# The last output copied in two column halves, a branch hint ahead of the end, and four accumulator banks for the last group

## The chip, the core and the metric

The kernel runs on one core of a Trainium2 chip. The engines that compute are TensorE (PE in the profile; its weight loads are PEld), VectorE (DVE), ScalarE (ACT) and GpSimd (POOL); SyncE (SP) issues the transfers. The metric is the device time of one execution in microseconds. A kernel's time is the median of its runs.

## What is computed

A gated linear recurrence over 768 steps for 4 x 8 heads of width 48, followed by a feed-forward layer on its output (3072 tokens, 384 wide, 2048 hidden):

```python
f = 1.0 / (1.0 + np.exp(-f_logit))
for t in range(S):
    state = f[:, :, t, :, None] * state + np.einsum('bhd,bhe->bhde', k[:, :, t], v[:, :, t])
    y[:, :, t] = np.einsum('bhd,bhde->bhe', q[:, :, t], state)
x = y.transpose(0, 2, 1, 3).reshape(B * S, H * D)
h = x @ w_in
g = h * np.tanh(np.log1p(np.exp(h)))      # for h > 20: h * tanh(h)
out = g @ w_out
```

## The kernel before

**Recurrence.** The sequence is cut into 24 chunks (6 in time, 4 batches) of 128 steps. A chunk is four steps in the code: `attn0` (loads `l`, `k`, `q`, `v`, the decays on ACT and DVE, the scores), `attn1`, `attn2`, `attn3` (the outputs, written as a high and a low part into `xt`). Its matmuls write the PSUM tiles `at0`, `at1`, `at2`.

**Feed-forward.** The tokens form 6 groups of 512 columns, the hidden width 16 blocks. One pair of group and block is a unit, 96 in all. A unit is `moe_in` (9 matmuls, L234, into a PSUM tile `h`), `mish` (nine steps, L244 to L252: four ACT passes, three DVE passes, then the high part `gh` on ACT and the low part `gl` on POOL), and `moe_out` (9 matmuls, L257, three into each of the PSUM tiles `o0`, `o1`, `o2`). There are two tiles `h`, two each of `n` and `g`, three each of `gh` and `gl`. The weights of a block are loaded once (`raw`, 768 KB) and split into a high and a low part (`split_w`, L336 to L346) on ACT and DVE. When a group is done, `out_unit` copies `o0` and `o2` with DVE (L619) and `o1` with ACT (L615) into `ob`, and SP sends each copy to `out` (L621). All transfers are issued from SP.

**What sets the order.** No engine's order is written by hand. Each step is added to a `Plan` with its engine, an assumed cost, and the names of what it reads and writes. `order()` packs all steps several times, forwards and backwards, then tries 100 variations of the ranks drawn from a fixed seed, keeps the best by its own model, and issues every engine's instructions in that order. So a step with another cost or another dependence can move instructions anywhere in the program. While the model sees PE idle before the first `moe_out`, it issues matmuls with zeros (`idle`, L326).

**The end.** A general path, for data whose decays are too strong, follows the planned part. `check` counts the good decays into `flag`; at L656 every engine loads `flag` into a register, at L657 it branches past the general path, whose instructions lie in between. After the branch each engine waits for its own work (SP for the eight semaphores of the transfers) and then for the others (L798).

Of the kernel before, what the change touches and what calls it, by code (L numbers as in the profile page):

```python
# [2 lines left out]

# [10 lines left out]
AF = mybir.ActivationFunctionType  # L14
# [5 lines left out]
P = 128  # L20
# [7 lines left out]
GT = GC * C  # L28
NG = NT // GT
NF = DFF // P  # L30
NK = DM // P
# [15 lines left out]
class Plan:  # L47
# [12 lines left out]
    def add(self, engine, cost, issue, reads=(), writes=(), size=0, port=False):  # L60

        n = len(self.steps)
        before = {self.writer[r] for r in reads if r in self.writer}
        for w in writes:
            before |= set(self.readers.get(w, ()))
            before |= {self.writer[w]} if w in self.writer else set()
        for r in reads:
            self.readers.setdefault(r, []).append(n)
        for w in writes:
            self.writer[w], self.readers[w] = n, []  # L70
        before.discard(n)
        self.steps.append((engine, cost, issue, before, size, port or engine == "pool"))
# [117 lines left out]
def recurrence_moe_kernel(  # L190
# [12 lines left out]
    nc = tc.nc  # L203
# [5 lines left out]
    def ctile(shape, dtype, name):  # L209
        return const.tile(shape, dtype, tag=name, name=name)  # L210
# [13 lines left out]
    flag = ctile([1, 1], I32, "flag")  # L224
# [5 lines left out]
    def moe_in(h, xt, j, wih=wih, wil=wil):  # L230
        n = 0
        for a in range(NK):
            for w, x in ((wih, 0), (wih, 1), (wil, 0)):
                nc.tensor.matmul(  # L234
                    h, w[:, j, a * P : (a + 1) * P], xt[:, x, a, :], start=(n == 0), stop=(n == 3 * NK - 1)
                )
                n += 1


    def mish(h, n, g, gh, gl):  # L240

# [20 lines left out]
    with tc.tile_pool(name="work", bufs=1) as pool, tc.tile_pool(  # L262
        name="psum", bufs=1, space=PSUM
    ) as psum:
        def ring(name, n, shape, dtype=F32, space=pool):
            return [space.tile(shape, dtype, tag=f"{name}{i}", name=f"{name}{i}") for i in range(n)]

        l_, k_, q_ = (ring(nm, NR, [P, NP, C]) for nm in "lkq")
# [5 lines left out]
        xt_ = ring("xt", 2, [P, 2, NP, GT], F32R)  # L274
        n_, g_ = (ring(nm, 2, [P, GT]) for nm in "ng")
        gh_, gl_ = (ring(nm, 3, [P, GT], F32R) for nm in ("gh", "gl"))
        ob_ = ring("ob", 3, [P, GT])
        raw_ = ring("raw", 2, [P, W_TILE, 2], I32)
        wt_ = ring("wt", 2, [P, W_TILE], I32)
        at_, h_, o_ = (ring(nm, n, [P, GT], F32, psum) for nm, n in (("at", 3), ("h", 2), ("o", NK)))  # L280
# [3 lines left out]
        add = plan.add  # L284
# [3 lines left out]
        def pairs(name, ps=range(NP)):  # L288
            return [(name, p) for p in ps]
# [277 lines left out]
        units = [(t, g, j) for t, (g, j0, j1) in enumerate(turns) for j in range(j0, j1)]  # L567

        def attend_goal(u):

            per = 4 * GC
            goal = per
            for a, b in LEAD + [(NF * g - 2, NF * (g + 1) - 2) for g in range(2, NG - 1)]:
                goal += min(per, max(0, per * (u + 1 - a) // (b - a)))
            return goal
# [13 lines left out]
        def out_unit(u):  # L589
            t, g, j = units[u]  # L590
            half = g < 2
            first, last = (j == x for x in (turns[t][1], turns[t][2] - 1))
            part = last and half and j == NF - 1
            gs = u % 3
            if part:
                for m in range(NK):
                    add("sp", 500, lambda m=m, g=g: nc.sync.dma_start(ob_[m], halves[g][m * P : (m + 1) * P, :]),
                        [("half", g, m)], pairs(("ob", m)), 262)
            if u == 0:
                plan.until = len(plan.steps)  # L600
            if last or first:
                for m in range(NK):
                    add("pe", 702, lambda m=m: moe_out(o_[m], m, gh_[gs], gl_[gs], j, first, last),
                        [("w", "h", j), ("w", "l", j), ("gh", gs), ("gl", gs)], [("o", m)])
            else:
                add("pe", 2106, lambda: [moe_out(o_[m], m, gh_[gs], gl_[gs], j, first, last) for m in range(NK)],
                    [("w", "h", j), ("w", "l", j), ("gh", gs), ("gl", gs)], [("o", m) for m in range(NK)])
            if last:
                dst = halves[g] if j < NF - 1 else out[:, g * GT : (g + 1) * GT]
                for m in range(NK):  # L610
                    if part:
                        add("dve", T_DVE(GT), lambda m=m: nc.vector.tensor_tensor(ob_[m], o_[m], ob_[m], ALU.add),
                            [("o", m)], pairs(("ob", m)))
                    elif m == 1:
                        add("act", T_ACT(GT, True), lambda m=m: nc.scalar.activation(ob_[m], o_[m], AF.Copy),  # L615
                            [("o", m)], pairs(("ob", m)))
                    else:

                        add("dve", T_DVE(GT), lambda m=m: nc.vector.tensor_copy(ob_[m], o_[m]),  # L619
                            [("o", m)] + ["flag"] * (u == len(units) - 1), pairs(("ob", m)))  # L620
                    add("sp", 500, lambda m=m, dst=dst: nc.sync.dma_start(dst[m * P : (m + 1) * P, :], ob_[m]),  # L621
                        pairs(("ob", m)), [("half", g, m) if half else ("out", g, m)], 262)

        split = 0
        for u in range(len(units) + LAG):
            if u < len(units):
                t, g, j = units[u]
                if j == split:
                    split_w(j)
                    split += 1  # L630
                x, hs, us, gs = g % 2, u % 2, u % 2, u % 3
                xk = [(hl, ("xt", x, c), p) for hl in "hl" for c in range(GC) for p in range(NK)]
                h = h_[hs]
                add("pe", 2106, lambda h=h, x=x, j=j: moe_in(h, xt_[x], j), xk + [("w", "h", j), ("w", "l", j)], [("h", hs)])
                kh, kn, kg = ("h", hs), ("n", us), ("g", us)
                ops = mish(h, n_[us], g_[us], gh_[gs], gl_[gs])
                rw = (
                    ([kh], [kn]), ([], [kn]), ([], [kn]), ([kh, kn], [kg]), ([kn], [kh]), ([], [kh]),
                    ([kh], [kg]), ([kg], [("gh", gs)]), ([kg, ("gh", gs)], [("gl", gs)]),
                )  # L640
                for (e, c, shared, fn), (r, w) in zip(ops, rw):
                    add(e, c, fn, r, w, port=shared)
            while done < min(4 * NCH, attend_goal(u)):
                attend()
            if u == len(units):
                check()
            if u >= LAG:
                out_unit(u - LAG)

        plan.idle = idle  # L650
        with tc.manual_schedule():
            plan.issue()


    total = P * NCH * NP
    good = nc.values_load(flag[0:1, 0:1], min_val=0, max_val=total)  # L656
    with tc.If(good < total):  # L657


        xs = dram.tile([DM, NT], F32, tag="xs", name="xs")  # L660
        with tc.tile_pool(name="slow", bufs=1) as pool, tc.tile_pool(
# [9 lines left out]
            with tc.For_i(0, B, 1) as b:  # L671
                with tc.For_i(0, NP, 1) as p:
                    f, k, q = (st([P, NCB, C], nm) for nm in ("sf", "sk", "sq"))
# [7 lines left out]
                    with tc.For_i(0, D, 1) as e:  # L681
# [13 lines left out]
                        for i in range(2):  # L695
                            ps = psum.tile([2, S // 2], F32, tag=f"sp{i}", name=f"sp{i}")
                            s = slice(i * S // 2, (i + 1) * S // 2)
# [9 lines left out]
            with tc.For_i(0, NG, 1) as g:  # L707
                x = st([P, NK, GT], "sx")
# [10 lines left out]
                n, g_ = (st([P, GT], nm) for nm in ("sn", "sg"))  # L719
                gh, gl = (pool.tile([P, GT], F32R, tag=nm, name=nm) for nm in ("sgh", "sgl"))  # L720
# [82 lines left out]
```

## Time and profile before

| | us |
|---|---|
| median of 3 runs | 522.92 |
| lowest, highest | 519.78, 523.32 |
| the profiled execution's own time | 521.81 |
| its span in the profile | 520.0 |
| PE, DVE, ACT busy of the span | 506.1, 370.4, 415.1 |
| granted TensorE clock | 0.999 |

The span runs from the first to the last instruction; 1.8 us of the execution lie outside it. "Idle before" in a row is the time in which the engine did nothing just ahead of the instructions of the row, with what ended it. A name with q (SPq, DVEq) is the engine's sequencer: it loads registers, branches and waits. A matmul's busy time overlaps the next one's.

### The profile page before, as it was taken

To read this page: it belongs to the slowest core of one execution; us is meant where nothing else is said; L and a number is where in the kernel's file an instruction comes from. 1 tells how busy PE (TensorE), PEld (TensorE's weight loads), DVE (VectorE), ACT (ScalarE), POOL (GpSimd) and SP (SyncE) were. 2 spreads that over 40 slices of the span, in tenths; PEclk is the share of its full clock that TensorE was granted. 3 is DMA by queue.
4 is the path that set the end of the run, shared out by engine and by line. 5 is a ranking of instruction groups with operands and counts; after the bars stand their busy time and mean duration, and the time that the engine had idled before them with its cause. 6 is when DMAs were issued, how large, how long until landed. Compare 5 with 4: busy or idle time off the path is not lost.

```text
span 520.0 us, 12828 instructions
## 1 busy us (share of the span) xinstructions
PE 506.1 (97%) x5258; PEld 399.3 (77%) x5258; DVE 370.4 (71%) x592; ACT 415.1 (80%) x731; POOL 155.1 (30%) x134
## 2 busy tenths in 40 slices
PE   8889899999999999999999999999999999999995
PEld 6667678777778778777777778778787787878884
DVE  3799999999998876856767667675667564554451
ACT  6888888988989978888778788877778785777771
POOL 1321533333322323233223222323231222232321
PEclk9999999999999999999999999999999999999999
DMA  8977534524601633411213321130220000010001
GB/s 278 335 236 261 202 122 154 161 83 140 220 18 34 201 100 98 134 57 33 82 33 94 111 78 45 43 97 17 61 64 1 3 2 32 0 61 1 1 1 66
DMA packets 22625, 48.86 MB, mean 94 GB/s; under 512 B 2656, under 2 KB 3808, under 8 KB 22560
## 3 DMA queue, kind: packets, MB, share of 16 engines
q1 hardware_dynamic: 22560, 47.98, 28.1%
q8 instruction: 42, 0.69, 0.6%
q14 instruction: 23, 0.19, 0.1%
HBM read 39.32 MB, written 6.29 MB: 88 GB/s over the span
## 4 chain that ended last, share of the span: by engine, by line
PE 73%; DVE 11%; ACT 8%; issue 3%; DMA 3%; SPq 1%; DVEq 0%; ACTq 0%
PE h L234 32%; PE o L257 32%; DVE g L250 2%; PE at L457 2%; PE at L504 2%; PE at L492 2%; DVE n L246 2%; DVE g L247 2%; DVE wt L341 2%; DMA l<-ft 1%; PE at L414 1%; PE at L439 1%; DMA raw<-ww 1%; ACT h L248 1%; ACT n L244 1%
## 5 line engine op out<-in xcount | busy, mean ns | idle before, releaser
L252 POOL TENSOR_TENSOR gl<-g,gh 128x512 fp32r<-128x512 f32 x96 | 128.2, 1336 | 294.3 <-ACT gh L251 262.7
L234 PE MATMUL h<-xt,wh 128*128 128x512 f32 x576 | 185.0, 402 | 1.6 <-DVE g L250 1.5
L234 PEld LDWEIGHTS h<-xt,wh 128*128 128x128 f32 x576 | 104.9, 188 | 29.2 <-DVE g L250 4.7
L257 PE MATMUL o<-gh,wh 128*128 128x512 f32 x288 | 116.2, 403 | 0.0
L234 PE MATMUL h<-xt,wl 128*128 128x512 f32 x288 | 113.7, 395 | 0.0
L257 PE MATMUL o<-gh,wl 128*128 128x512 f32 x288 | 113.7, 395 | 0.0
L257 PE MATMUL o<-gl,wh 128*128 128x512 f32 x288 | 113.7, 395 | 0.0
L246 DVE SCALAR_TENSOR_TENSOR n<-n 128x512 f32<-128x512 f32 x96 | 67.1, 699 | 59.8 <-ACT n L245 59.7
L244 ACT ACTIVATE n<-h,hcap 128x512 f32<-128x512 f32 x96 | 65.8, 685 | 34.2 <-PE h L234 33.4
L250 DVE TENSOR_TENSOR g<-g,h 128x512 f32<-128x512 f32 x96 | 65.4, 681 | 33.5 <-ACT h L249 32.9
L248 ACT ACTIVATE h<-n,two 128x512 f32<-128x512 f32 x96 | 66.0, 687 | 18.6 <-DVE g L247 18.6
L251 ACT ACTIVATE gh<-g 128x512 fp32r<-128x512 f32 x96 | 60.3, 628 | 19.2 <-DVE g L250 15.2
L247 DVE TENSOR_TENSOR g<-h,n 128x512 f32<-128x512 f32 x96 | 66.1, 689 | 8.7 <-POOL gl L252 1.3
L245 ACT ACTIVATE n<-n,hcap 128x512 f32<-128x512 f32 x96 | 69.2, 721 | 2.2
L257 PEld LDWEIGHTS o<-gh,wh 128*128 128x128 f32 x288 | 54.0, 187 | 13.6 <-issue 0.3
L257 PEld LDWEIGHTS o<-gl,wh 128*128 128x128 f32 x288 | 54.0, 187 | 13.3
L234 PEld LDWEIGHTS h<-xt,wl 128*128 128x128 f32 x288 | 54.0, 187 | 13.2
L257 PEld LDWEIGHTS o<-gh,wl 128*128 128x128 f32 x288 | 54.1, 188 | 12.0
L249 ACT ACTIVATE h<-h 128x512 f32<-128x512 f32 x96 | 56.0, 583 | 1.7
L383 DVE TENSOR_TENSOR_SCAN cum<-go,l 128x512 f32<-128x512 f32 x20 | 26.7, 1334 | 0.0
L420 DVE TENSOR_TENSOR a<-at,causal 128x256 f32<-128x256 f32 x44 | 17.8, 417 | 9.7 <-PE at L414 9.5
L520 POOL TENSOR_TENSOR state<-tmp,ends 128x256 f32<-128x256 f32 x20 | 16.7, 835 | 21.6 <-PE at L492 17.4
(103 smaller groups left out, 504.4 us busy)
## 6 DMA issues: line engine op xcount, KB each, us to landing
raw<-ww SPq DMA_DIRECT2D x16, 768.0 KB, 4.9
v<-vn SPq DMA_DIRECT2D x24, 256.0 KB, 3.8
k<-kk SPq DMA_DIRECT2D x23, 256.0 KB, 3.3
q<-qq SPq DMA_DIRECT2D x23, 256.0 KB, 3.8
l<-fl SPq DMA_DIRECT2D x20, 256.0 KB, 2.7
out<-ob SPq DMA_DIRECT2D x18, 256.0 KB, 2.6
xt<-xt SPq DMA_DIRECT2D x15, 128.0 KB, 2.1
half<-ob SPq DMA_DIRECT2D x6, 256.0 KB, 2.5
```

The lines of the kernel that those rows point to most:

```text
L234: nc.tensor.matmul(h, w[:, j, a * P : (a + 1) * P], xt[:, x, a, :], start=(n == 0), stop=(n == 3 * NK - 1))
L244: ("act", T_ACT(GT, True, 1), 0, lambda: nc.scalar.activation(u, h, AF.Relu, bias=hcap, scale=-1.0)),
L245: ("act", T_ACT(GT, False, 1), 0, lambda: nc.scalar.activation(u, u, AF.Exp, bias=hcap, scale=-1.0)),
L246: ("dve", T_DVE(GT), 1, lambda: nc.vector.scalar_tensor_tensor(n, u, 2.0, u, ALU.add, ALU.mult)),
L247: ("dve", T_DVE(GT), 0, lambda: nc.vector.tensor_tensor(g, h, n, ALU.mult)),
L248: ("act", T_ACT(GT, False, 1), 0, lambda: nc.scalar.activation(h, n, AF.Ln, bias=two)),
L249: ("act", T_ACT(GT, True), 0, lambda: nc.scalar.activation(h, h, AF.Exp, scale=-1.0)),
L250: ("dve", T_DVE(GT), 0, lambda: nc.vector.tensor_tensor(g, g, h, ALU.mult)),
L251: ("act", T_ACT(GT), 0, lambda: nc.scalar.activation(gh, g, AF.Copy)),
L252: ("pool", T_POOL(GT), 1, lambda: nc.gpsimd.tensor_tensor(gl, g, gh.bitcast(F32), ALU.subtract)),
L257: nc.tensor.matmul(o, w[:, j, m * P : (m + 1) * P], x, start=(first and i == 0), stop=(last and i == 2))
L383: add("dve", 2 * T_DVE(w) - 70, lambda s=s, cum=cum: nc.vector.tensor_tensor_scan(cum.rearrange("p a c -> p (a c)"), go[:, s].rearrange("p ...
```

## The change

Four edits, all in the planned part:

- In the last group's last unit the copy of `o2` becomes two copies of 256 columns. ACT copies the upper half and issues its transfer from its own queue; DVE copies the lower half, SP issues that transfer. Both steps now name `flag` as read; before, only the two full copies on DVE did. The three `moe_out` parts of that unit are tied to the order `o0`, `o1`, `o2`.
- In the last group (units 80 to 95) four tiles serve as `h` (the two and `at0`, `at1`), four as `n` (with `l0`, `l1`) and four as `g` (with `k0`, `k1`).
- The general path gets a name, and a hint that the branch past it is likely taken is placed on ACT, DVE and POOL behind the first instruction each has in the last unit's `mish`, and on SP behind the first transfer of the group before the last.
- The plan is made anew with these steps.

```diff
@@ out_unit
+            end = u == len(units) - 1
...
-                        [("w", "h", j), ("w", "l", j), ("gh", gs), ("gl", gs)], [("o", m)])
+                        [("w", "h", j), ("w", "l", j), ("gh", gs), ("gl", gs)] + [("o", m - 1)] * (end and m > 0), [("o", m)])
...
+                    elif end and m == NK - 1:
+
+                        def part_out(eng, s, m=m, dst=dst):
+                            if eng is nc.sync:
+                                nc.vector.tensor_copy(ob_[m][:, s], o_[m][:, s])
+                            else:
+                                nc.scalar.activation(ob_[m][:, s], o_[m][:, s], AF.Copy)
+                            eng.dma_start(dst[m * P : (m + 1) * P, s], ob_[m][:, s])
+
+                        for e, t_copy, eng, x in (("act", T_ACT(GT // 2, True), nc.scalar, 1), ("dve", T_DVE(GT // 2), nc.sync, 0)):
+                            add(e, t_copy, lambda eng=eng, x=x: part_out(eng, slice(x * GT // 2, (x + 1) * GT // 2)),
+                                [("o", m), "flag"], [("ob", m, x)])
+                        continue
                     else:
-
                         add("dve", T_DVE(GT), lambda m=m: nc.vector.tensor_copy(ob_[m], o_[m]),
-                            [("o", m)] + ["flag"] * (u == len(units) - 1), pairs(("ob", m)))
-                    add("sp", 500, lambda m=m, dst=dst: nc.sync.dma_start(dst[m * P : (m + 1) * P, :], ob_[m]),
+                            [("o", m)], pairs(("ob", m)))
+                    add("sp", 500, partial(mark, "sp" if g == NG - 2 else "", lambda m=m, dst=dst: nc.sync.dma_start(dst[m * P : (m + 1) * P, :], ob_[m])),
...
+        free = NF * (NG - 1)
+        hs_ = [(h, ("h", i)) for i, h in enumerate(h_)] + [(at_[i], ("at", i)) for i in range(2)]
...
+        def mark(e, fn):
+            ins = fn()
+            marks.setdefault(e, ins)
...
-                x, hs, us, gs = g % 2, u % 2, u % 2, u % 3
+                us = u % 2 if u < free else u % 4
+                x, gs = g % 2, u % 3
...
+                    if u == len(units) - 1:
+                        fn = partial(mark, e, fn)
...
+        for e, ins in marks.items():
+            if e:
+                with tc.issue_after(ins.ins):
+                    tc.mark_branch_hint_location("general", "LikelyTaken", engines=[ins.ins.engine])
...
-    with tc.If(good < total):
+    with tc.If(good < total, label="general"):
```

Line numbers in the changed program are one higher up to L592, and 2 to 36 higher behind it. Three places show what the new plan moves. First SP, at the start of the program (`l` decays' inputs, `raw` a weight block, `k`, `q`, `v` a chunk's inputs). Before:

```order
L355 DMA l_82<-ft 128x512
L355 DMA k_84<-kk 128x256
L355 DMA q_87<-qq 128x256 x2
L358 DMA v_90<-vn 128x512
L336 DMA raw_122<-ww 128x1536
L355 DMA k_85<-kk 128x512
L355 DMA l_83<-ft 128x512
L355 DMA q_88<-qq 128x512
```

Now:

```order
L356 DMA q_87<-qq 128x256 x2
L359 DMA v_90<-vn 128x512
L356 DMA l_83<-ft 128x512
L337 DMA raw_122<-ww 128x1536
L356 DMA k_85<-kk 128x512
L356 DMA q_88<-qq 128x512
```

The third chunk's `l_83` is now issued ahead of the first weight block; before, it stood behind it.

Second DVE, around the first unit's last pass (`g` with the tile `h`, L250, now L251). Before:

```order
L346 TENSOR_TENSOR wl_62<-wt0_124,wh_61 128x768 [waits Activation_49]
L250 TENSOR_TENSOR g0_111<-g0_111,h0_129 128x512 [waits Activation_49]
L537 TENSOR_TENSOR xt1_108<-at1_127,xt1_108 128x2x128 [waits Activation_49]
L246 SCALAR_TENSOR_TENSOR n1_110<-n1_110 128x512
L341 SCALAR_TENSOR_TENSOR wt1_125<-raw1_123,wt1_125 128x768 [waits DMAHW5_49,DVE_49]
L537 TENSOR_TENSOR xt1_108<-at0_126,xt1_108 128x2x128 [waits Activation_49]
L247 TENSOR_TENSOR g1_112<-h1_130,n1_110 128x512 [waits DVE_49]
```

Now:

```order
L247 SCALAR_TENSOR_TENSOR n1_110<-n1_110 128x512 [waits Activation_49]
L341 TENSOR_SCALAR wt1_125<-wt1_125 128x768
L251 TENSOR_TENSOR g0_111<-g0_111,h0_129 128x512 [waits DVE_49,Activation_49]
L344 SCALAR_TENSOR_TENSOR wt0_124<-raw0_122,wt0_124 128x768
L476 TENSOR_TENSOR tmp1_106<-at1_127,mid1_104 128x256 [waits DVE_49,PE_49,Pool_49]
L248 TENSOR_TENSOR g1_112<-h1_130,n1_110 128x512 [waits DVE_49]
L421 TENSOR_TENSOR a3_102<-at1_127,causal_66 128x256
```

The second unit's first pass (`n1`) and its second (`g1`) have moved ahead of passes of the weight split and of `xt`. Counted over the whole list, the last pass of units 0 to 9 was DVE's row 69, 79, 85, 96, 100, 114, 117, 124, 130 and 137; now it is row 65, 72, 80, 90, 98, 111, 117, 122, 127 and 134. At unit 19 it is row 195 in both. On ACT the `gh` of units 0 to 9 was row 91, 102, 106, 119, 123, 135, 137, 148, 155 and 163, and is now row 89, 97, 107, 116, 124, 134, 141, 147, 154 and 162.

Third the end, DVE and then ACT. DVE before:

```order
L250 TENSOR_TENSOR g1_112<-g1_112,h1_130 128x512 [waits DVE_49,Activation_49]
L619 COPY ob0_119<-o0_131 128x512 [waits DMAHW0_49,PE_49]
L619 COPY ob2_121<-o2_133 128x512 [waits DMAHW2_49,PE_49]
L656 TENSOR_LOAD flag_71 [waits DVE_49]
```

Now:

```order
L834 BRANCH_PREFETCH_HINT
L251 TENSOR_TENSOR k0_84<-k0_84,at0_126 128x512 [waits DVE_49,Activation_49]
L248 TENSOR_TENSOR k1_85<-at1_127,l1_82 128x512 [waits DVE_49,Pool_49]
L251 TENSOR_TENSOR k1_85<-k1_85,at1_127 128x512 [waits DVE_49,Activation_49]
L588 CAST flag_71<-at2_128 1x1 [waits PE_49]
L633 COPY ob0_119<-o0_131 128x512 [waits DMAHW1_49,PE_49]
L623 COPY ob2_121<-o2_133 128x256 [waits DMAHW2_49,Activation_49]
L692 TENSOR_LOAD flag_71 [waits DVE_49]
```

ACT before:

```order
L251 ACTIVATE gh2_115<-g1_112 128x512 [waits DVE_49,PE_49,Pool_49]
L615 ACTIVATE ob1_120<-o1_132 128x512 [waits DMAHW1_49,PE_49]
L656 TENSOR_LOAD flag_71 [waits DVE_49]
```

Now:

```order
L252 ACTIVATE gh2_115<-k1_85 128x512 [waits DVE_49,PE_49,Pool_49]
L617 ACTIVATE ob1_120<-o1_132 128x512 [waits DMAHW0_49,PE_49]
L625 ACTIVATE ob2_121<-o2_133 128x256 [waits DMAHW2_49,PE_49]
L626 DMA out<-ob2_121 128x256 [waits DMAHW5_49,Activation_49]
L692 TENSOR_LOAD flag_71 [waits DVE_49]
```

DVE's half copy waits for ACT's half copy, not for PE; the cast of `flag` has moved from the middle of the last group to just ahead of DVE's last copies.

In the middle of the program the order of PE has changed too: at the first `moe_out` matmul of a unit, the `moe_in` of 3 more units than of finished `moe_out` had been issued in 27 of units 0 to 31 before (of 4 in five), and of 4 to 6 in 31 of the 32 units 48 to 79; now it is 3 in 26 of these 32 and 4 in six. The zero matmuls of L326 are 29 (before: 32).

## Rows read from the trace of the kernel before

**Rows 1.** The page, its first part: busy time, share of the span and instructions of an engine.

```profile
PE 506.1 (97%) x5258; PEld 399.3 (77%) x5258; DVE 370.4 (71%) x592; ACT 415.1 (80%) x731; POOL 155.1 (30%) x134
```

**Rows 2.** Busy time by stretch: the stretch, its length, then busy us and instructions of each engine, the granted clock, the DMA engines' share and GB/s.

```profile
26.00:65.00 39.00, 35.39 (x783) 27.21 (x771) 38.06 (x60) 32.63 (x64) 13.10 (x11) 1.00 0.69 233
65.00:160.00 95.00, 94.50 (x693) 73.59 (x670) 91.12 (x129) 84.85 (x142) 31.54 (x23) 1.00 0.38 124
...
160.00:514.10 354.10, 354.07 (x3472) 281.04 (x3470) 226.30 (x377) 278.22 (x484) 104.13 (x85) 1.00 0.17 54
...
100.00:150.00 50.00, 49.87 (x346) 39.25 (x345) 48.18 (x66) 43.71 (x70) 16.33 (x12) 1.00 0.43 137
200.00:250.00 50.00, 50.00 (x545) 39.78 (x544) 34.78 (x60) 40.63 (x72) 14.12 (x12) 1.00 0.24 75
```

**Rows 3.** What PE waited for between 26 and 160 us, the first two lines: us in total, times, longest.

```profile
PE h L234 <- DVE g L250: 1.5, 4, 0.8
PE o L533 <- ACT xt L530: 0.8, 1, 0.8
```

**Rows 4.** The zero matmuls (L326) alone, by stretch: PE's busy time and records (two a matmul), then PEld's.

```profile
26.00:40.00 14.00, 5.50 (x22) 3.81 (x22) 1.00 0.72 240
40.00:65.00 25.00, 4.69 (x18) 2.72 (x16) 1.00 0.68 229
65.00:100.00 35.00, 0.00 (x0) 0.00 (x0) 1.00 0.40 133
```

**Rows 5.** The chain of work that ended last, followed back from 30 us: start, us, what. The load `l<-ft` is `l_83`.

```profile
5.45 7.22 DMA l<-ft
12.69 1.04 DVE l L373
...
14.41 0.72 ACT l L375
15.15 0.60 ACT kt L442
```

**Rows 6.** The timeline near the end, the first and the last step of the last unit's `mish`: start, us, engine, line, instruction.

```profile
503.60 0.69 ACT L244 ACTIVATE n<-h,hcap 128x512 f32<-128x512 f32 x1 [0.65 <-PE h L234]
...
509.93 1.29 POOL L252 TENSOR_TENSOR gl<-g,gh 128x512 fp32r<-128x512 f32 x1 [0.65 <-ACT gh L251]
```

**Rows 7.** The chain of work that ended last, its end.

```profile
503.56 10.52 PE o L257 x45
514.08 0.02 issue
514.10 0.69 DVE ob L619
```

**Rows 8.** Busy time by stretch as in Rows 2, behind the last matmul.

```profile
514.25:516.40 2.15, 0.00 (x0) 0.00 (x0) 0.55 (x1) 0.00 (x0) 0.00 (x0) 1.00 0.99 360
516.40:517.30 0.90, 0.00 (x0) 0.00 (x0) 0.00 (x0) 0.00 (x0) 0.00 (x0) 1.00 0.11 41
```

**Rows 9.** The instructions of the branch, L657, on each sequencer: duration in ns (least, median, most), start of the first and the last.

```profile
L657 SPq EVENT_SEMAPHORE  x8: 17/17/17, 518.1 to 518.7; - x8
L657 POOLq COMPARE_BRANCH  x1: 45/45/45, 510.4 to 510.4; - x1
L657 POOLq EVENT_SEMAPHORE  x1: 17/17/17, 511.3 to 511.3; - x1
...
L657 ACTq COMPARE_BRANCH  x1: 50/50/50, 513.9 to 513.9; - x1
...
L657 ACTq EVENT_SEMAPHORE  x1: 17/17/17, 514.4 to 514.4; - x1
L657 DVEq COMPARE_BRANCH  x1: 72/72/72, 515.0 to 515.0; - x1
L657 SPq COMPARE_BRANCH  x1: 50/50/50, 515.2 to 515.2; - x1
L657 DVEq EVENT_SEMAPHORE  x1: 21/21/21, 518.5 to 518.5; - x1
```

**Rows 10.** The same view of the loads of `flag` (L656) and of the program's end (L798).

```profile
L656 SPq TENSOR_LOAD <-flag x1: 731/731/731, 457.0 to 457.0; - x1
...
L656 DVEq TENSOR_LOAD <-flag x1: 818/818/818, 514.1 to 514.1; - x1
...
L798 SPq EVENT_SEMAPHORE  x10: 17/28/28, 518.7 to 520.0; - x10
```

**Rows 11.** SP's own waits from 514 us on (us in total, times, longest), and the transfer issued from 514.5 us on: KB, us from issue to landing.

```profile
SPq L657 <- SPq L657: 2.9, 1, 2.9
...
SPq L621 <- DVE ob L619: 0.4, 1, 0.4
...
out<-ob SPq DMA_DIRECT2D x1, 256.0 KB, 2.8
```

**Rows 12.** Groups of instructions by line and shape: count, busy us, mean ns, idle before.

```profile
L619 DVE COPY ob<-o 128x512 f32<-128x512 f32 x12 | 8.2, 685 | 4.8 <-PE o L257 4.8
...
L537 DVE TENSOR_TENSOR xt<-at,xt 128x256 fp32r<-128x256 f32 x40 | 16.1, 418 | 9.3 <-ACT xt L530 9.0
...
L530 ACT ACTIVATE xt<-at 128x256 fp32r<-128x256 f32 x44 | 15.1, 378 | 1.3 <-PE at L504 1.2
```

More of the change, by code (lines that the diff above doesn't have):

```diff
@@ L1 @@
 import random
+from functools import partial
 from contextlib import ExitStack
@@ L616, in out_unit @@
                             [("o", m)], pairs(("ob", m)))
+                    elif end and m == NK - 1:
[9 more added lines that the diff above has]
+                        continue
                     else:
                         add("dve", T_DVE(GT), lambda m=m: nc.vector.tensor_copy(ob_[m], o_[m]),
-                            [("o", m)] + ["flag"] * (u == len(units) - 1), pairs(("ob", m)))
-                    add("sp", 500, lambda m=m, dst=dst: nc.sync.dma_start(dst[m * P : (m + 1) * P, :], ob_[m]),
+                            [("o", m)], pairs(("ob", m)))
+                    add("sp", 500, partial(mark, "sp" if g == NG - 2 else "", lambda m=m, dst=dst: nc.sync.dma_start(dst[m * P : (m + 1) * P, :], ob_[m])),
                         pairs(("ob", m)), [("half", g, m) if half else ("out", g, m)], 262)
+        free = NF * (NG - 1)
+        hs_ = [(h, ("h", i)) for i, h in enumerate(h_)] + [(at_[i], ("at", i)) for i in range(2)]
+        ns_, gs_ = (
+            [(x, [(nm, i)]) for i, x in enumerate(r)]
+            + [(x.rearrange("p a c -> p (a c)"), pairs((rn, i))) for i, x in enumerate(rest[:2])]
+            for nm, r, rn, rest in (("n", n_, "l", l_), ("g", g_, "k", k_))
+        )
+        marks = {}
+        def mark(e, fn):
+            ins = fn()
+            marks.setdefault(e, ins)
         split = 0
@@ L630, in recurrence_moe_kernel @@
                     split += 1
-                x, hs, us, gs = g % 2, u % 2, u % 2, u % 3
+                us = u % 2 if u < free else u % 4
+                x, gs = g % 2, u % 3
                 xk = [(hl, ("xt", x, c), p) for hl in "hl" for c in range(GC) for p in range(NK)]
[L633 to L636, printed above, removed]
+                (h, kh), (n, kn), (g_t, kg) = hs_[us], ns_[us], gs_[us]
+                add("pe", 2106, lambda h=h, x=x, j=j: moe_in(h, xt_[x], j), xk + [("w", "h", j), ("w", "l", j)], [kh])
+                ops = mish(h, n, g_t, gh_[gs], gl_[gs])
                 rw = (
-                    ([kh], [kn]), ([], [kn]), ([], [kn]), ([kh, kn], [kg]), ([kn], [kh]), ([], [kh]),
-                    ([kh], [kg]), ([kg], [("gh", gs)]), ([kg, ("gh", gs)], [("gl", gs)]),
+                    ([kh], kn), ([], kn), ([], kn), ([kh] + kn, kg), (kn, [kh]), ([], [kh]),
+                    ([kh], kg), (kg, [("gh", gs)]), (kg + [("gh", gs)], [("gl", gs)]),
                 )
                 for (e, c, shared, fn), (r, w) in zip(ops, rw):
+                    if u == len(units) - 1:
+                        fn = partial(mark, e, fn)
                     add(e, c, fn, r, w, port=shared)
```

## The prediction

> **What bounds the kernel now.** The page's first part comes first: PE is busy 97% of the span, no other engine over 80% [rows 1]. The busy time by stretch says where the 3% lie. From 65 us to the last matmul PE stands still for 0.5 us in all (94.50 of 95.00 and 354.07 of 354.10), so what moves on the other engines there is hidden [rows 2]. Time can change in two places only: the head, up to 65 us, and the tail behind 514.1 us.
>
> In the head two limits are close together. From 26 to 65 us DVE is busy for 38.06 of 39.00 us, PE for 35.39, and 5.50 + 4.69 us of PE's share are zero matmuls that compute nothing [rows 2, 4]. What PE waits for longest is the in-order work of these two: DVE's last `mish` pass, 1.5 us, and ACT's `xt`, 0.8 us [rows 3].
>
> The tail is 520.0 - 514.1 = 5.9 us. The chain ends with 45 `moe_out` matmuls in a row and the DVE copy of `o2`, over at 514.8 [rows 7]. What follows is on no engine's busy account, so I read the sequencers. SP branches at 515.2 and runs its next instruction at 518.1; DVE branches at 515.0 and goes on at 518.5. ACT needs 0.5 us for the same step, POOL 0.8 [rows 9]. SP's own wait list has this as a wait of SP for SP, 2.9 us, which no transfer explains: the last transfer, issued at 514.8, has landed 2.8 us later, at 517.6 [rows 11]. Behind 518.5 come semaphores and the end, until 520.0 [rows 10]. So the tail is bound by the late instructions behind two branches, and 0.5 to 0.9 us ahead of that by the last landing.
>
> **The change part by part.** *The hint.* It adds one sequencer instruction on each of four engines; on DVE and ACT it stands where they idle (ACT 0.65 us just ahead of the last unit [rows 6]), so it costs nothing; without that cover it would be some 0.02 us, as a semaphore, to 0.8 us, as a register load [rows 9, 10]. If the code behind the branch is there in time, SP goes on 0.5 to 0.8 us after its branch, as ACT and POOL do, and finds the last transfer not landed. Next late is that landing, 517.6. Before, from the later of the eight semaphores, near 518.5, to the end took 1.5 us [rows 9, 10]. From 517.6 plus a wake-up of about 0.05 the same 1.4 to 1.5 us give 519.1: **-0.9 us**. The bounds are 0 (the hint does nothing, or DVE or SP alone stays late) and -1.0.
>
> By the Trainium skill (Runtime: NRT & Kernel Launch, section Instruction fetch mechanics) prefetch is purely sequential, and a taken branch whose target isn't in the current two-page window forces a fetch before execution goes on. The gaps of SP and DVE agree with it, and the short ones of ACT and POOL fit a target inside the window; no run here shows an address. Taken literally the rule leaves a hint nothing to do, and the sum would be 520.7, as in the first rival below.
>
> *The halves.* DVE's half copy waits for ACT's half, as the order shows, so they run one behind the other: about 0.38 + 0.42 us by the 128x256 rows that read PSUM [rows 12], with some 0.05 between, in place of 0.69. The second half's transfer is issued some 0.15 us later than the whole was. It does not matter either way: from 514.25 to 516.40 the DMA engines are busy for 0.99 of the time at 360 GB/s [rows 8], which is the 768 KB of the last three copies in one stream. ACT's half is in the queue before that stream runs dry, SP's half (issue near 514.95, first byte some 0.8 us later as for the first of the three: issue 513.4, stream 514.25) too. The bytes end at 516.4, the landing stays at 517.6: **0**, between -0.2 and +0.3. Had the halves been spread over two idle queues, nothing else would have come of it: the stream is one.
>
> `flag` is cast later, but still ahead of DVE's first last copy, 1.4 us before the end of PE's work; SP then needs 0.73 us for its load [rows 10], which now stands between its last group's transfers, and is done before the copies are. Behind it are three transfers that wait for those copies anyway: 0, and at worst the 0.73 us if the cast slipped to the end.
>
> *Four tiles in the last group.* PE is at work without a gap there (354.07 of 354.10), the `mish` of the last unit takes 503.56 to 511.2, and its `gl` is wanted by the third of the last nine matmuls, at 514.08 - 7 x 0.234 = 512.4 (10.52 / 45 = 0.234 us each) [rows 6, 7]; in the new order five units of `moe_out` again follow the last `moe_in`. Nothing to gain: 0. Lost cover would show as a wait of `moe_out` for `gl`, at most the 1.3 us of one POOL pass [rows 6].
>
> *The new plan in the head.* This is the largest term and the least sure. DVE runs about 38.06 / 60 = 0.63 us an instruction there [rows 2]. The last pass of units 0 to 9 comes 4, 7, 5, 6, 2, 3, 0, 2, 3 and 3 rows earlier, and level at unit 19. PE stops waiting around units 3 to 5 (65 to 80 us), where the lead is 6, 2, 3 rows: 3.8, 1.3, 1.9 us. ACT (32.63 / 64 = 0.51 us a row) has its `gh` earlier by 3, -1, 1 rows there, and four rows later at unit 6, 2.0 us. Three zero matmuls fewer take 6 records of 0.25 us away, 1.5 us [rows 4], but they stood where PE would wait. `l_83` leaves its place behind a weight block: its chain, which held ACT's in-order `kt` until 15.15 [rows 5], can move up by as much as the 768 KB take at the stretch's rate, some 2 us, yet the chunk ahead loads its `k` and `q` no earlier. I take the two smaller DVE leads, mean 1.6, less 0.5 for an ACT row: **-1.1 us**. Bounds: -3.8 (the lead of unit 3 in full) and +2.0 (ACT's delay at unit 6 in full).
>
> *The new plan in the middle.* `moe_in` no longer runs 4 to 6 units ahead but 3. With 3 ahead in units 8 to 22 the old kernel kept PE busy 49.87 of 50 us while DVE was at 48.18 [rows 2], so 3 is enough: 0.
>
> The sum: -0.9 + 0 - 1.1 + 0 = -2.0 us against the profiled execution's own 521.81 (span 520.0 and 1.8 around it): **519.8 us**. That execution lies 1.1 us under the median of 522.92 and inside the 3.5 us that the three runs span, so I leave the sum as it is. 1%, 5.2 us, is about what a measurement of this kernel can tell from no change; the forecast is a gain of less than half of that.
>
> **The rivals.** *Only the tail or only the head.* The hint doesn't bring the code in time on both SP and DVE. For it: no such instruction is in the trace, so no row shows that it fetches, and SP's stands some 60 us ahead of its branch (the group before the last went out when `flag` was loaded, 457.0 [rows 10]). Against it: ACT and POOL pass the same branch in 0.5 and 0.8 us, so the code can be near. The tail then gives 0: 521.81 - 1.1 = 520.7.
>
> *The head gives more.* DVE is the bound up to 65 us at 97.6%, the lead counts in full, and the early load adds to it: -3.8 - 0.9 and up to 1.5 for the zero matmuls: 515.6 to 517.
>
> *Slower: the lead of 3 is too short.* From the last `moe_in` to the last `gl` the uncontended chain takes 503.56 to 511.22, 7.7 us [rows 6, 7]; three units' distance gives PE about 8.4 us of other matmuls (36 of 0.234 us). If the chunks' work on ACT and DVE lengthens the chain past 8.4 us, PE waits in each such unit, where before 4 to 6 units covered it. Units 23 to 79 are 57; an excess of 0.15 us in each is 8.5 us: 519.8 + 8.5 = 528. It decides from a mean chain of 8.4 us. Against it: DVE has 34.78 and ACT 40.63 of 50 us in that part, less than where 3 sufficed (48.18 and 43.71) [rows 2].
>
> **How the numbers follow.** The forecast as summed 0.58, only one of the two gains 0.22, the large gain 0.13, the slower middle 0.07. Range: the bounds of head and tail from the sum, -3.8 - 1.0 and +2.0 + 0.3, are 516.8 to 524.1; the upper end needs no gain in the tail and the worst head at once, so I stop at 523.2, and the lower goes to 516.5 for half of the large gain. Over 1% faster would be under 517.7: 0.12. Over 1% slower is the last rival alone, with its larger half: 0.05. Within 1%: 0.83.
>
> **What would show it.** The branch of SP and DVE followed within 1 us by the next instruction, with the end set by a landing some 3.5 us behind the last matmul: the hint works. The span behind the last matmul near 5.0 us, from 5.9. The two half copies one behind the other, the DMA share still near 1 over some 2.1 us. The last matmul near 513, with PE's idle time and zero matmuls up to 65 us smaller by about a microsecond; PE without a gap from 160 us on. I am wrong if PE shows waits for `gl` in the middle, if the head ends later than before, or if a branch still costs 3 us.

## The result, and the profile after

| | before | after |
|---|---|---|
| median of 6 runs each, us | 521.68 | 526.31 |
| lowest, highest | 519.78, 523.32 | 525.56, 528.52 |
| the profiled execution, its span | 521.81, 520.0 | 528.35, 526.5 |
| last matmul ends, from there to the end of the span | 514.07, 5.96 | 519.83, 6.66 |

The ratio is 1.008 with an interval of 1.0052 to 1.0108: 0.8% slower, 4.6 us by the medians. Forecast were 519.8 and at most 523.2. In the two profiled executions PE ends 5.8 us later and the tail is 0.7 us longer.

The stretches, with the columns of [rows 2] and the answer to its first three lines; the last line is a piece of the first:

```profile
26.00:65.00 39.00, 35.86 (x682) 27.58 (x681) 36.57 (x55) 31.36 (x62) 10.72 (x10) 0.96 0.64 207
65.00:160.00 95.00, 90.35 (x722) 69.86 (x721) 90.55 (x126) 79.67 (x132) 29.84 (x23) 1.00 0.39 132
160.00:519.80 359.80, 359.52 (x3493) 285.02 (x3491) 235.15 (x384) 280.51 (x495) 106.42 (x86) 1.00 0.17 54
...
51.64:55.05 3.41, 3.39 (x11) 2.89 (x11) 3.41 (x7) 2.55 (x5) 1.08 (x1) 0.50 0.02 5
```

From 65 to 160 us PE now stands still for 4.65 us, before for 0.50; behind 160 us for 0.28 in 360. ACT is busy there for 5.2 us less than before. DVE is busy about as long (90.55 of 95.00 us against 91.12) but gets only 126 instructions done, before 129: it is still the engine that bounds this stretch, and its instructions take longer on average. What PE waited for from 26 to 160 us, as in [rows 3]:

```profile
PE at L440 <- DVE mid L474: 3.2, 2, 2.2
PE h L235 <- DVE g L251: 2.5, 4, 0.9
```

The zero matmuls, now L327, as in [rows 4]; they take about as much of PE as before:

```profile
26.00:40.00 14.00, 5.92 (x24) 3.83 (x23) 1.00 0.71 240
40.00:65.00 25.00, 4.70 (x15) 2.96 (x13) 0.93 0.60 189
```

The longest single wait, in the timeline (start, us, engine, line, instruction, idle time before):

```profile
48.17 1.27 POOL L294 TENSOR_TENSOR k<-k,inv 128x512 f32<-128x512 f32 x1 [5.10 <-ACT inv L391]
48.21 2.04 DVE L342 SCALAR_TENSOR_TENSOR wt<-raw,wt 128x768 int32<-128x768 int32 x1
...
51.11 0.40 DVE L474 TENSOR_TENSOR mid<-state,at 128x256 f32<-128x256 f32 x1
...
51.66 1.08 PE L440 MATMUL at<-ident,k 128*128 128x128 f32 x4 [2.21 <-DVE mid L474]
```

A pass of the weight split that usually takes 0.95 us starts together with POOL's multiplication of `k` and takes 2.04. Behind it in DVE's queue stands `mid`, and PE's transposes for the next chunk write the tile `at` that `mid` still has to read. PE idles 2.21 us, of which the 1.09 us of that pass's lengthening are half, and as it starts again the granted clock is 0.50 (1.2 GHz) for 3.41 us, where it had been 1.00 (2.4 GHz).

The passes of the weight split from 65 to 160 us in the changed kernel: count, busy us, mean ns, idle before:

```profile
L342 DVE SCALAR_TENSOR_TENSOR wt<-raw,wt 128x768 int32<-128x768 int32 x10 | 12.5, 1247 | 0.0
L347 DVE TENSOR_TENSOR wl<-wt,wh 128x768 fp32r<-128x768 f32 x11 | 12.1, 1097 | 0.4 <-ACT wh L346 0.4
L344 DVE SCALAR_TENSOR_TENSOR wt<-raw,wt 128x768 int32<-128x768 int32 x10 | 11.4, 1144 | 0.0
L341 DVE TENSOR_SCALAR wt<-wt 128x768 int32<-128x768 int32 x10 | 8.9, 892 | 0.0
```

The 41 passes of the same kinds in the kernel before:

```profile
L341 DVE SCALAR_TENSOR_TENSOR wt<-raw,wt 128x768 int32<-128x768 int32 x10 | 11.8, 1181 | 0.0
L346 DVE TENSOR_TENSOR wl<-wt,wh 128x768 fp32r<-128x768 f32 x11 | 11.8, 1073 | 0.0
L343 DVE SCALAR_TENSOR_TENSOR wt<-raw,wt 128x768 int32<-128x768 int32 x10 | 10.5, 1053 | 0.0
L340 DVE TENSOR_SCALAR wt<-wt 128x768 int32<-128x768 int32 x10 | 7.5, 747 | 0.0
```

44.9 us against 41.6: 3.3 us longer, on the engine that bounds this stretch. Other instructions of DVE give about half of this back, as they were the longer ones before. The scan `cum` in the same stretch, before and now:

```profile
L383 DVE TENSOR_TENSOR_SCAN cum<-go,l 128x512 f32<-128x512 f32 x2 | 3.7, 1856 | 0.0
L384 DVE TENSOR_TENSOR_SCAN cum<-go,l 128x512 f32<-128x512 f32 x2 | 2.6, 1302 | 0.0
```

Over all of DVE's instructions ahead of 160 us, the time above the median length of the same instruction in the same profile comes to 13.8 us before and 14.6 in the changed kernel. So the new order hardly adds to the lengthening there. What it changes is which instructions are lengthened, and so who waits for them.

The tail, as in [rows 9] (the branch is now L693):

```profile
L693 SPq EVENT_SEMAPHORE  x8: 17/17/17, 524.6 to 525.1; - x8
L693 DVEq COMPARE_BRANCH  x1: 84/84/84, 520.9 to 520.9; - x1
L693 SPq COMPARE_BRANCH  x1: 70/70/70, 521.1 to 521.1; - x1
L693 DVEq EVENT_SEMAPHORE  x1: 21/21/21, 521.7 to 521.7; - x1
```

DVE goes on 0.8 us behind its branch (before 3.5), SP 3.5 us (before 2.9). One late branch is left, and it sets the end.

### The profile page after: what moved, and what is told of

The parts are those of the page before. It is cut to its first block, busy times and chain, and to the rows that moved or that the text cites. A ratio compares the mean times of both kernels' runs of the same rounds, so it can differ in the third digit from the quotient of the medians.

```text
span 526.5 us, 12819 instructions
## 1 busy us (share of the span) xinstructions
PE 507.9 (96%) x5252; PEld 399.6 (76%) x5252; DVE 376.7 (72%) x592; ACT 411.7 (78%) x732; POOL 153.0 (29%) x134
## 4 chain that ended last, share of the span: by engine, by line
PE 71%; DVE 11%; ACT 7%; issue 4%; DMA 4%; SPq 1%; POOL 0%; DVEq 0%; ACTq 0%; POOLq 0%
PE o L258 31%; PE h L235 27%; PE at L235 3%; PE at L458 2%; PE at L505 2%; PE at L493 2%; PE at L440 2%; DVE g L251 2%; DVE g L248 2%; DVE wt L342 2%; PE at L415 1%; DMA k<-kk 1%; DVE n L247 1%; DVE wt L344 1%; DMA raw<-ww 1%
## 5 line engine op out<-in xcount | busy, mean ns | idle before, releaser
L253 POOL TENSOR_TENSOR gl<-g,gh 128x512 fp32r<-128x512 f32 x88 | 116.5, 1325 | 280.2 <-ACT gh L252 267.4
L235 PE MATMUL h<-xt,wh 128*128 128x512 f32 x528 | 169.3, 401 | 2.7 <-DVE g L251 2.7
L235 PEld LDWEIGHTS h<-xt,wh 128*128 128x128 f32 x528 | 96.7, 188 | 28.2 <-DVE g L251 5.9
L235 PE MATMUL h<-xt,wl 128*128 128x512 f32 x264 | 104.3, 395 | 0.0
L249 ACT ACTIVATE h<-n,two 128x512 f32<-128x512 f32 x88 | 60.5, 688 | 36.0 <-DVE g L248 35.5
L251 DVE TENSOR_TENSOR g<-g,h 128x512 f32<-128x512 f32 x88 | 60.1, 683 | 39.8 <-ACT h L250 38.7
L245 ACT ACTIVATE n<-h,hcap 128x512 f32<-128x512 f32 x88 | 60.1, 683 | 25.9 <-PE h L235 25.4
L248 DVE TENSOR_TENSOR g<-h,n 128x512 f32<-128x512 f32 x88 | 60.6, 688 | 6.3
L246 ACT ACTIVATE n<-n,hcap 128x512 f32<-128x512 f32 x88 | 63.3, 719 | 1.5
L250 ACT ACTIVATE h<-h 128x512 f32<-128x512 f32 x88 | 51.3, 583 | 1.6
L538 DVE TENSOR_TENSOR xt<-at,xt 128x256 fp32r<-128x256 f32 x40 | 16.3, 418 | 14.7 <-ACT xt L531 14.5
```

The lines of the kernel that those rows point to most:

```text
L235: nc.tensor.matmul(h, w[:, j, a * P : (a + 1) * P], xt[:, x, a, :], start=(n == 0), stop=(n == 3 * NK - 1))
```

## The experiments: which part of the change costs the time

The theory to be tried: the new plan's order costs the time, between 45 and 160 us, and none of the other three edits does. The rival: those edits themselves.

**Two tiles in place of four.**

```diff
-                us = u % 2 if u < free else u % 4
+                us = u % 2
```

> The changed kernel with two tiles instead of four in the last group; the halves, the later flag and the hint stay. Its steps then stand in exactly the order of the kernel before. Theory (the re-drawn order costs the time, in the stretch from 45 to 160 us): PE ends within 0.5 us of the kernel before, at 514.1, the tail behind it stays as in the changed kernel, 6.7 us, so 0.7 more than before: median near 522.4, ratio 1.000 to 1.003. Rival (the halves, the flag's place or the hint cost the time): about 526, ratio 1.008.

522.15 against 521.90 for the kernel before on the same chip, ratio 1.0009 (0.9987 to 1.0031). The 4.6 us are gone, with halves and hint still in. From 65 to 160 us:

```profile
65.00:160.00 95.00, 94.43 (x668) 73.51 (x667) 91.19 (x129) 84.69 (x141) 31.25 (x23) 1.00 0.38 124
```

The tail is 5.93 us, not the 6.7 expected, so halves and hint together change nothing there. The last transfer is issued at 514.7 and lands 1.9 us later, at 516.6, which is 2.8 us behind the last matmul. Before it was 3.6, but in the changed kernel, with the same halves, it is 3.7, so these runs don't show that the halves bring the landing forward. In all three SP goes on behind its branch later than the last landing, and so hides it.

**Four tiles, old order.** The planner is told of two tiles, the instructions use four.

```diff
-                (h, kh), (n, kn), (g_t, kg) = hs_[us], ns_[us], gs_[us]
+                h, n, g_t = hs_[us][0], ns_[us][0], gs_[us][0]
+                kh, kn, kg = hs_[u % 2][1], ns_[u % 2][1], gs_[u % 2][1]
```

> The changed kernel with its four tiles, but with the order of the kernel before: the planner is told of two tiles in the last group, the instructions use four. Theory (the order costs the time): as with two tiles, median near 522.4, ratio 1.000 to 1.003, no stop of PE in the last group. Rival (the use of other tiles itself costs, or the order does nothing): about 526, ratio 1.008.

522.46, ratio 1.0006 (0.9984 to 1.0028). The tiles cost nothing that can be told from noise. The loss comes with the order that the planner draws once it knows of four.

**Another draw for the kernel before, and one for the changed kernel.** In each, one line changes the start of the planner's random numbers:

```diff
-        pick = random.Random(1)
+        pick = random.Random(6)
```

> The kernel before with another start of the random numbers by which the planner tries orders, and nothing else. The planner's own end for that order is 506.93 us against 506.91 for the kernel before (506.04 for the changed one). Theory (any re-drawn order moves the time by some us, which the planner's end does not foretell): another time than before by 1 to 6 us, in either direction, made before 200 us. Rival (the four tiles did it, and a mere re-draw is harmless): within 0.5 us of before.

521.08, ratio 0.9987 (0.9973 to 1.0000): 0.8 us under before by the medians, hardly more than this can tell, and between the theory's least effect of 1 us and the rival's 0.5. This run decides nothing, except that a new draw needn't matter much. In the changed kernel, with `Random(3)`:

> The changed kernel with another start of the random numbers by which the planner tries orders. The planner's own end is 505.82 us, the lowest of all (changed kernel 506.04, before 506.91). Theory (the time is that of the order drawn, and the planner's end doesn't foretell it): another time than 526 by over 1 us. Rival (four tiles always cost 4 us): 526 within 0.7. Were the planner's end a guide, it would be the fastest, near 521.

520.03, ratio 0.9952 (0.9929 to 0.9975): 2.7 us under before by the medians of that comparison, some 6 under the changed kernel. It is the fastest of the versions that compute everything and were timed more than once. PE's idle time from 65 to 160 us is 0.61 us:

```profile
65.00:160.00 95.00, 94.39 (x746) 73.80 (x745) 90.36 (x130) 85.08 (x144) 32.76 (x23) 1.00 0.37 124
```

So four tiles don't have to cost 4 us. Whether they have a part in this gain, or the order alone makes it, no run shows. The planner's end does not sort the orders: it put the changed kernel 0.9 us ahead of before, and the chip has it 4.6 behind.

## The experiments: why that order is slow

Theory A: DVE's passes over SBUF (the on-chip memory in which the tiles outside PSUM lie) are lengthened beside POOL, and this order puts more of them there, in front of what PE waits for. Rival B: the order makes engines wait, whatever POOL does. Rival C, formed after the first pair: POOL's own tiles come late.

**POOL's passes over an eighth of their columns**, in the kernel before and in the changed one, alike; the order stays. The rest of the columns is left out, except in the first pass into each tile of `gl` and into each batch's state.

```diff
-            ("pool", T_POOL(GT), 1, lambda: nc.gpsimd.tensor_tensor(gl, g, gh.bitcast(F32), ALU.subtract)),
+            ("pool", T_POOL(GT), 1, lambda: low(gl, g, gh)),
...
+            if on_pool:
+                dst, x, y = (t[:, :, : C // 8] for t in (dst, x, y))
```

> The kernel before with POOL's passes (the low part gl, k times inv, the state) over an eighth of their columns, so that POOL is hardly beside DVE; the rest of the columns keeps what stood there. The order is unchanged. With the next run it separates two causes. Cause A: DVE's passes over SBUF are lengthened beside POOL, and the re-drawn order puts more of them there (by the two traces 9.3 us of lengthening before, 19.3 after). Cause B: the order itself makes engines wait. By either this one is as fast as before or up to 2 us faster: 519.5 to 522.

> The changed kernel with POOL's passes over an eighth of their columns, the order unchanged. By cause A its distance to the kernel before with the same cut shrinks from 4.4 us to under 1.5; by cause B it stays at 3 us or more.

520.01, ratio 0.9963 (0.9935 to 0.9992), and 519.42, ratio 0.9931 (0.9906 to 0.9956). The distance between the orders is gone: -0.6 us where it was +4.6. B falls. PE's idle time from 65 to 160 us in the changed order is 1.27 us, from 4.65:

```profile
65.00:160.00 95.00, 93.73 (x744) 73.84 (x742) 84.44 (x129) 86.18 (x145) 7.58 (x23) 1.00 0.36 125
```

This doesn't separate A from C, as a short pass is also done early.

**The same with POOL's time filled.** Behind each short pass ten (for the state five) memsets of one column into the same tile are to fill the time.

```diff
+        fill(gl[:, 0:1].bitcast(F32), 10 if c.stop < GT else 0)
```

> The changed kernel with POOL's passes over an eighth of their columns, and behind each of them ten (state: five) memsets of one column into the same tile, 98 ns each, so that POOL hands its tiles over as late as in the changed kernel (0.34 + 1.0 us against 1.33) and yet hardly touches memory beside DVE. Cause A (DVE's passes are lengthened beside POOL): as fast as with the short passes alone, 519.4 within 1.2. Cause C (POOL's passes come late to PE): as slow as the changed kernel, 525 to 527.

523.05, ratio 1.0009 (0.9990 to 1.0027): between what A and what C forecast. DVE's passes from 65 to 160 us nearly have their own length again. The same 41 as above take 36.3 us, so at least 8.6 of the changed kernel's 44.9 were lengthening:

```profile
L363 DVE TENSOR_TENSOR wl<-wt,wh 128x768 fp32r<-128x768 f32 x11 | 10.5, 951 | 0.1
...
L358 DVE SCALAR_TENSOR_TENSOR wt<-raw,wt 128x768 int32<-128x768 int32 x10 | 10.4, 1036 | 0.0
...
L360 DVE SCALAR_TENSOR_TENSOR wt<-raw,wt 128x768 int32<-128x768 int32 x10 | 9.6, 964 | 0.0
L357 DVE TENSOR_SCALAR wt<-wt 128x768 int32<-128x768 int32 x10 | 5.8, 580 | 0.3 <-ACT wt L355 0.3
```

But the filling is too long. A `gl` with its ten memsets holds POOL for 1.88 us (median), a whole pass for 1.30:

```profile
101.65 0.32 POOL L250 TENSOR_TENSOR gl<-g,gh 128x64 fp32r<-128x64 f32 x1 [2.78 <-ACT ends L411]
102.03 1.50 POOL L245 MEMSET gl<- 128x1 f32 x10
```

So POOL's tiles come later here than in the changed kernel, and PE waits for them longer. In the first 26 us it waits 1.6 us for `k`, in the changed kernel 0.6:

```profile
PE at L456 <- POOL k L245: 1.6, 1, 1.6
```

Two stretches of this run; the granted clock of the first is 0.95, with the short passes alone it was 1.00:

```profile
0.00:26.00 26.00, 21.08 (x338) 16.53 (x342) 14.28 (x28) 18.55 (x43) 6.28 (x35) 0.95 0.85 304
...
65.00:160.00 95.00, 93.23 (x735) 72.00 (x735) 85.32 (x132) 84.05 (x140) 32.05 (x239) 1.00 0.39 132
```

By the ratios, 1.0080 to 1.0009, the lengthening costs this order at least 0.7% or 3.7 us, since the late tiles cost more in this run than in the changed kernel. The rest, 1.0009 to 0.9931 or 4.1 us, is the price of late tiles and of the clock in this run. The clock is a part of it: among the executions with a mean granted clock of 0.997 or more the medians are 525.8 for the changed kernel, 521.5 with the filled and 519.4 with the short passes (4, 4 and 5 executions, not all on the same chip). How much C costs the changed kernel itself is read from its own profile. From 26 to 160 us PE waits for POOL only this much:

```profile
PE o L258 <- POOL gl L253: 0.3, 1, 0.3
```

So A holds for the stretch where PE lost its time (idle 4.65, 1.77 and 1.27 us in the three), and C is small there. Only A's "more of them" is not borne out: the amount of lengthening ahead of 160 us is nearly that of before (13.8 and 14.6 us above), and the place is another. One run is missing: the order of before with filled passes. From whole to short passes that order gained 0.4%, 1.9 us, and the new order 1.5%, 7.8 us; how the 1.9 divide between lengthening and late tiles is open.

## The experiments: the hint

**No hint at all** in the changed kernel (its loop over `marks` is left out):

> The changed kernel without its hints, everything else and the order as it is. In its profile DVE went on 0.8 us after its branch; with the same hint and the old order it took 3.0 us. Theory (the hint does nothing; whether the code behind the branch is at hand is a matter of where it lies): DVE again within 1 us, SP again 3 to 3.5 us, time as the changed kernel, 526 within 0.7. Rival (DVE's hint worked): DVE takes 3 us or more and goes on after SP, the end some 0.5 us later.

526.48 against 522.75 for before on that chip, ratio 1.0082 (1.0050 to 1.0114), as with the hints. DVE takes 3.35 us, so from this run alone the hint seemed to have worked. SP takes 3.3 us, where it took 3.5 with the hint:

```profile
L693 SPq EVENT_SEMAPHORE  x8: 17/17/17, 520.9 to 521.5; - x8
L693 SPq COMPARE_BRANCH  x1: 50/50/50, 517.6 to 517.6; - x1
L693 DVEq COMPARE_BRANCH  x1: 72/72/72, 517.8 to 517.8; - x1
L693 DVEq EVENT_SEMAPHORE  x1: 21/21/21, 521.1 to 521.1; - x1
```

This profile has PE idle for 4.48 us from 65 to 160 us at a granted clock of 1.00 from 26 us on, so the fall of the clock in the changed kernel's profile may or may not come; the order loses its time without it:

```profile
26.00:65.00 39.00, 36.67 (x691) 28.40 (x692) 38.26 (x56) 32.24 (x62) 12.96 (x11) 1.00 0.68 227
65.00:160.00 95.00, 90.52 (x724) 70.19 (x723) 90.78 (x128) 81.81 (x135) 29.23 (x23) 1.00 0.38 125
```

**SP's hint later**, with two tiles:

```diff
-partial(mark, "sp" if g == NG - 2 else "", ...
+partial(mark, "sp" if g == NG - 1 else "", ...
```

> As the first, with SP's hint some 58 us later: behind the first transfer of the last group, about 1.8 us ahead of SP's branch, where it stood some 60 us ahead. Theory (a hint that stands too early does nothing): SP goes on within 1 us of its branch, where it took 3.4 us, the last landing then sets the end, and the time is 1.0 to 1.6 us under that of the first: near 521.0, ratio 0.997 to 0.999. Rival (on SP the hint does nothing wherever it stands): SP takes 3 us again and the time is that of the first.

523.13, ratio 1.0025 (0.9998 to 1.0052). SP took 2.9 us, though its hint ran at 514.9, 1.5 us ahead of the branch. DVE, with its hint, took 3.1 us here and 3.0 in the first run, where it took 0.8 in the changed kernel. The theory of the early hint falls. Next suspect: where hint and branch stand in the program.

**SP's branch further along**, by 14 transfers of four bytes, with the third seed:

> The order of the third seed, 520.03, with 14 transfers of four bytes put on SP's queue after the outputs of group 3, where SP idles, so that SP's hint and branch stand 14 transfers further along in its program. DVE's hint shortened its branch in two kernels where hint and branch stand at instruction 820 and 833 or 827 and 838 of DVE's program and not in two where they stand at 817 and 828 or 815 and 826. Theory (the place in the program decides whether a hint helps): SP goes on within 1 us of its branch, where it took 2.8, the last landing sets the end, and the tail falls from 6.0 to about 5.2: near 519.3. Rival (SP's hint never helps): SP takes 2.7 to 3.5 us again and the time is 520.0 within 0.5.

520.94, ratio 0.9970 (0.9953 to 0.9986), not told apart from the third seed alone. SP takes 2.8 us again:

```profile
L699 SPq EVENT_SEMAPHORE  x8: 17/17/17, 517.4 to 518.0; - x8
L699 SPq COMPARE_BRANCH  x1: 70/70/70, 514.6 to 514.6; - x1
```

**DVE's branch further along**, by six memsets of one column, with two tiles; then by seven and without the hints:

> The changed kernel with two tiles (order of before), and six memsets of one column on DVE behind group 3's first output, so that DVE's hint and branch stand at instruction 823 and 834. Theory (the place decides): DVE goes on within 1 us of its branch, where it took 3.0 us with the hint at 817 and the branch at 828. Rival (it is something else in the new orders): 3.0 us again. The time stays at 522 either way, since SP ends last.

> As the last run (two tiles, memsets on DVE behind group 3's first output), but with seven memsets and without the hints, so that DVE's branch stands at instruction 834 of its program again. Theory (it takes both, the hint and the place): DVE takes 3 us or more behind its branch. Rival (the place alone decides, the hint is idle): DVE goes on within 1 us, as with the hint. SP takes about 3 us by either, so the time stays near 522.

518.45 and 520.37 in single executions, which tell nothing by themselves. DVE goes on 0.6 us behind its branch in both. With the hint:

```profile
L699 DVEq COMPARE_BRANCH  x1: 84/84/84, 510.9 to 510.9; - x1
...
L699 DVEq EVENT_SEMAPHORE  x1: 21/21/21, 511.5 to 511.5; - x1
```

Without:

```profile
L699 DVEq COMPARE_BRANCH  x1: 72/72/72, 513.0 to 513.0; - x1
...
L699 DVEq EVENT_SEMAPHORE  x1: 21/21/21, 513.6 to 513.6; - x1
```

So for DVE the place decides and the hint is idle: slow with it at instruction 826 and 828, quick without it at 834. Counted in all 14 profiles, DVE is slow with its branch at instruction 824, 826, 827, 828 or 832 of its program and quick at 833, 834 or 838. By this the changed kernel without its hints was slow because leaving out the hint moved the branch from 833 to 832. SP is slow in all 14, at 308 to 310 and at 324; whether there is a quick place for it is open.

What the place changes is seen on the queue that fetches instructions (packets, MB, share of the DMA engines). In the kernel with two tiles, from DVE's slow branch to the end, 515.15 to 519.7 us:

```profile
q14 instruction: 5, 0.04, 3.2%
```

In the last run, from DVE's quick branch to the end, 513.0 to 518.6 us:

```profile
q14 instruction: 4, 0.03, 2.0%
```

There the 0.6 us behind the branch, to 513.6 us, hold no fetch, but these rows only:

```profile
q10 hardware_dynamic: 110, 0.11, 53.8%
q1 hardware_dynamic: 8, 0.01, 5.5%
```

And from 511.0 to 512.98 us, ahead of that branch, one stands:

```profile
q14 instruction: 1, 0.01, 1.7%
```

All profiles agree: five such fetches from DVE's branch on and one in the 12 us ahead of it in the seven where DVE is slow, four and two in the seven where it is quick. Three of those behind the branch run in SP's gap in the quick case, too. The rows don't name the engine that fetched.

## Why the prediction was wrong

*The step that failed is the new plan in the head:* -1.1 us were forecast, and the order cost about 4 (0.7 to 0.8% by the ratios). The miss of 6.5 us is the 4.6 by which the medians differ and the 1.1 and 0.9 that were forecast and did not come. I read the leads of DVE's and ACT's rows as time gained, at a mean duration of a row, as if each instruction kept its length and its start followed from its rank. What the order sets besides is which passes of DVE run at the same time as POOL's. In the changed kernel lengthened passes stand ahead of what PE wants: it waited for `mid` and `g` for 3.2 and 2.5 us, where it had waited for `g` alone, 1.5, and from 65 to 160 us it stood still for 4.65 us, before for 0.5. With POOL's passes cut short the two orders are level (-0.6 us). The link from a lengthened pass to a wait was followed for the longest wait alone. The sums of the page before give no warning, but the trace does: of one of these passes the longest of 16 is over twice the median (least, median, longest in ns).

```profile
L341 DVE SCALAR_TENSOR_TENSOR wt<-raw,wt x16: 942/950/2050, 14.7 to 143.1; 128x768 int32<-128x768 int32 x16
```

My bound of +2.0 for the head came from a delay of ACT at one unit; no bound allowed for passes that get longer. And I looked for the effect up to 65 us, with leads up to 80, and took 65 to 160 as covered, since PE was at 94.50 of 95.00 there. That number says that nothing waits; it doesn't say how much may be lost before something does, with DVE at 91.12. (The lower bound of the range, 516.8, comes out only with the halves' -0.2, which its sentence doesn't name; without it, it is 517.0. It changes nothing.)

*The hint:* -0.9 forecast, 0 measured (tails of 5.96 and 5.93 us in the same order). The hint's part of my first rival, that it does nothing, was right; its time of 520.7 was not. The rule of the Trainium skill that stood beside it (Runtime: NRT & Kernel Launch, section Instruction fetch mechanics), by which a taken branch can have to wait for a fetch of instructions, agrees with the fetches inside the gaps; no run shows an address. I gave that rival 0.22 and the working hint 0.58 with no row that showed a hint at work. In the changed kernel SP's gap is 3.5 us, before 2.9, and the tail 0.7 us longer; over all profiles that gap lies between 2.7 and 3.6 us, and what sets it within that is open.

*The halves:* 0 was right as a time. They run one behind the other, as forecast. The landing did not stay at 3.6 us behind the last matmul: it came at 2.8 in the first run and at 3.7 in the changed kernel. SP's branch, which was expected to be out of the way, hid this.

*The late flag, the four tiles, the plan in the middle:* 0, as forecast: PE idles 0.28 us behind 160 us, and the order of before with four tiles is as fast as with two. The slower rival, too short a lead in the middle, did not come true, though its 528 was near the time: the loss lies ahead of unit 23, by another mechanism.

## What to carry to other kernels

A planner's order is a draw: an edit in the last group that the planner merely knows of re-orders the head, and the end that its model gives doesn't tell 520 from 526. Test the edit under the old order first, then draw several orders and time them. Where VectorE bounds a stretch, look at the longest against the median of each pass in the profile before counting ranks: here the gap was the price of a neighbour on another engine, and a new order changed which instructions paid it and who waited for them.

## What the runs showed of the hardware

DVE's 128x768 pass with two inputs in SBUF took 0.95 us in the median, up to 2.07 beside a POOL pass of 1.3 us that reads SBUF, and a mean of 0.95 to 1.04 where POOL ran memsets of one column and short passes. The Trainium skill states such an exclusive hold between the two engines (SBUF — State Buffer, section SBUF: two separate sides), only against a GpSimd operation that reads SBUF in the case of two inputs; the runs agree in both halves: the 2.04 us pass was lengthened by 1.09 beside a pass of 1.27, and memsets lengthened hardly anything. The time from a branch to DVE's next instruction was 3.0 to 3.6 us with the branch at instruction 824 to 832 of its program and 0.6 to 1.0 at 833 to 838, in seven profiles each.
